# A sketched-attention and gated-FFN kernel: a new hand-over order of its steps, element-wise steps moved from VectorE to GpSimd and back, and some small products split or joined

## The chip, the cores and the metric

The kernel runs on one core of a Trainium2 chip. The core has a matrix engine (TensorE, "PE" in the profile; its weight loads are listed as "PEld"), a vector engine (VectorE, "DVE"), an activation engine (ScalarE, "ACT"), a general engine (GpSimd, "POOL") and an engine that here only issues transfers (SyncE, "SP"). Each works through its own list of instructions in order and waits on the others through semaphores. Operands lie in a large on-chip memory (SBUF); products are written to a small accumulation memory (PSUM) of eight banks. The metric is the time of one execution on the device in microseconds, the median of several runs; lower is better.

## The reference

There are two parts, and the second takes the output of the first as its rows.

```python
a = einsum('rd,bhsd->bhsr', S1, x); b = einsum('rd,bhsd->bhsr', S2, x)   # S1, S2: 8 x 32
phi(x) = einsum('bhsi,bhsj->bhsij', a, b)            # 64 features per token and head
kv = einsum('bhsf,bhsd->bhfd', phi(k), v);  z = sum(phi(k), axis=2)
attn = (phi(q) @ kv) / (phi(q) @ z + 1e-6)
h = (x @ w1) * (x @ w2) @ w3;  out = h @ w_out       # x: 4352 x 128, d_ff = 1024
```

q, k and v have batch 4, 4 heads, 1088 tokens and a head width of 32. The weights and S1, S2 come as 64-bit floats, which the kernel turns into 32-bit ones itself. The denominator is a sum with much cancellation, so the kernel forms it from sums of two parts (a coarse part and a rest) where one 32-bit number would not do.

## The kernel before, in words

**Steps and their order.** `make_steps` defines 952 small named steps, each a few instructions. `ORDER` (L63 on) is a list of all their names, written out by hand or by a planner, and the instructions of every engine are chained in that order. So the list fixes the queue of each engine, the transfers of SP among them, and a step that has to wait holds up all that stands behind it on its engine. `SLOTS` says which buffer each tile gets, so a tile also waits for the last reader of the one before it in the buffer. `POOL` and `ACTS` are sets of step names: a step that calls `on(name)` runs on GpSimd or ScalarE if its name is in there, and on VectorE otherwise. `WARM` gives the number of idle products (128x128 zeros on 256 columns, L221) in each of 29 filler steps on TensorE.

**Names.** `s.*` prepares S1 and S2. `w0` to `w10` turn the weights into 32-bit numbers: two ScalarE passes (`.c`, `.m`), a shift (`.j`, L432) and two GpSimd additions (`.a0`, `.a1`, L438). w0 and w1 hold the two halves of w1 and w2, w2 holds w_out, w3 to w10 hold w3. `f0` to `f7` fold w3 into w_out (L471). For each batch entry b, `k{b}.*` builds what the keys contribute:

- `max`, `g`, `lead`, `rest` (L589) split k into a coarse part and a rest, tile `kk`;
- `gram` (L597) sums products of these into a 128x64 tile, `Gm` to `Gb` (L787 to L804) split that sum into `Ga` and `Gb`, `T0` and `T1` (L811, L816) multiply by S2, `Ta`, `Tb`, `Ts` split again, `N0`, `N1` (L849, L855) multiply by S1-products, and `Na`, `Nb` split a third time into the denominator's weights. `Nf`, `Nl`, `Nh`, `Nr` spread these over heads;
- `kT`, `ab`, `kp` (L615) form phi(k), `kv` (L707) and `kvr` (L714) sum it against v, `kqt`, `kq`, `kz` lay the result out.

`q{g}.*` does the same for the queries of one part: `tr` to `rm` (L927 to L947, L1246) split them, `A0`, `A1`, `C0`, `C1` are products with S and with the denominator's weights, `sm` to `sc` split and complete them, `p01`, `p2`, `p12`, `dn`, `de`, `rc` give the reciprocal of the denominator, `phi` (L1128, L1382) the features, and `pt`/`pT`, `x`, `xT` the 128 attention columns that the FFN reads. There are seven parts: q0 and q1 have 512 tokens of batch 0 and differ from the others, q2 and q3 are the halves of batch 1, q4 and q6 are wide parts of 1024 tokens for batches 2 and 3, qr holds the 64 last tokens of all batches.

`g{g}.{c}a`, `b`, `o` are the FFN for 512 tokens and one of eight blocks of d_ff: products with w1 (L1441) and w2 (L1451), a ScalarE copy `c` (L1446), the VectorE multiplication `m` (L1457), and the product with the folded w3 (L1464). g0 needs q0, g1 needs q1, g4 and g5 need q4, and so on; `gr` has 256 tokens and ends the kernel.

**What is around the change.** `q0.C0` (L973) makes its products with S as weights, 12 of them for a quarter of the tokens each, so that the result stands by feature and `C0t` turns it on VectorE. `k{b}.Gb` is two VectorE instructions: the rest of the Gram sum, then its second half added. `Tb` and `Ts` are three more of that kind. `N1` has four products with `P2b` as weights. A wide part's last products are two steps: `x0` (heads 0 and 1) after `pT0`, `x1` (heads 2 and 3) after `pT1`, with the innermost loop over heads:

```python
for i in range(2):                                                  # L1396
    for t in range(4):
        for h in range(u * H // parts, (u + 1) * H // parts):
```

The first PE steps of the order end with `... q1.C0 q0.xs q0.xt q0.xT k1.ab warm9 g0.3a`; from `g0.3a` on nearly all that TensorE does are FFN products with short groups of attention products between them.

Of the kernel before, what the change touches and what calls it, by code (L numbers as in the profile page):

```python
# [11 lines left out]
F32 = mybir.dt.float32  # L12
BF16 = mybir.dt.bfloat16
F16 = mybir.dt.float16
I32 = mybir.dt.int32
# [3 lines left out]
ALU = mybir.AluOpType  # L19
# [10 lines left out]
        "012345670124570215340653472634172531760170257252752376263752061072146121763501746235201471"  # L30
        "534625401624543730126730126743207041267314103742604132014632604176276315041761623041260354"
        "142350632610526107260132017426312647374014201702435034266716051645140571261045713654174653"
        "5434170251212",
    "k_g": "0101",
    "l": "0123456789abc021365749cb803a61725b49875130249ba68053c4b791a823b7904c83a2517",
    "m": 
        "0123456789abcdefghijklmnopqrstuv0413259867efmhgdjuto4b16cvpl0erqaofk8u1lcjn7g53edmvibs26q9"
        "h4fa8cjdot5pi30nrqmv97lkha1ibu3o8se26aubtpdfhc5lke3jest5fbcub0u692idarvsj91f286itkm47ovi5l"
        "ndc6p8e0tj",
    "q_m": "0101010",  # L40
    "raw": "012102101201201",
    "s": "012345671203615470231647053216470",
    "x": "012001210020",
}

WARM = [16, 10, 6] + [4] * 2 + [2] * 8 + [1] * 16
# [6 lines left out]
    k0.Nh k0.rest1 k1.kp0 k1.kp1 k2.kp0 k3.kp0 k3.kp1 k3.rest0 q0.p2 q0.phi1 q1.p12 q1.p2 q1.phi q2.al  # L53
    q2.p12 q2.p2 q2.phi0 q3.al q3.phi0 q4.phi0 q4.phi1 q6.al q6.phi1 qr.p2 qr.phi0 s.Pp s.blk s.blkh
    s.rest
# [6 lines left out]
c.zeros c.mask c.ident warm17 s.four k0.zero k0.loadr warm0 k0.load0 k0.load1 k0.max0 k0.max1 k0.g k0.lead0 s.load  # L62
k0.rest0 s.words warm3 k0.tr0 warm19 warm1 k0.gram0 k0.gram1 k0.lead1 k1.zero warm4 warm14 k0.tr1 s.pair s.low s.lead  # L63
s.sum s.rest s.T s.tc s.P q0.load k0.rest1 s.zero s.R k0.kT1 k0.gram2 q0.tr k0.gram3 k1.load q1.tr k1.loadr kr0.load
s.c q0.max k0.gram4 w1.load s.blk k1.max q0.l2 s.Pc k0.kT0 kr0.tr k0.ab1 k0.ab0 k0.Gm s.Pm s.blkh k0.Gt k1.g k0.Ga
q0.l1 q1.max k0.T0 k0.abc1 k0.Gb k0.T1 q1.l2 warm2 k0.kp1 warm21 warm7 k1.tr1 kr0.kT k0.abc0 k1.lead0 k0.Ta warm18
q0.A0 q1.l1 warm13 k0.kp0 warm28 k0.Tb kr0.ab kr0.abc k1.tr0 q0.rm s.Pp v0.zero k0.Ts k0.N0 k1.kT0 q0.C0 k1.rest0
v0.load q0.sma k0.N1 q0.sta k0.kv0 kr0.kp k0.kv3 v0.loadr k0.kv1 k0.kv2 k0.kvr k1.gram0 k1.gram1 k0.Na s.KS q0.sha
k0.Nr q0.C0t q0.sla k0.kvc k0.kvm warm5 warm12 q0.sca k0.Nf k0.Nb k1.kT1 k0.kzt k0.Nh k2.zero kr1.load kr1.tr q0.al
q0.phi0 q1.rm w0.load q0.A1 warm11 warm24 q1.A0 warm23 k0.kz kr1.kT kr1.ab warm16 k0.kqt warm22 warm6 k0.Nl q0.smy  # L70
q1.sm w1.c q0.sty k2.loadr q1.st q1.sh w0.c q0.pt0 warm10 q0.C1 q0.pc0 q0.shy k1.gram2 k1.gram3 q0.phi1 k1.gram4
q0.pt1 q0.C1t q0.pc1 w0.m q0.x0 q0.x1 q0.sly q0.p01 q0.scy q0.p2 q0.p12 q0.dn k1.Gm q0.de q0.rc w2.load q1.load q1.C0
w0.j q0.xs w0.a0 q1.sl k1.Gt q0.xt q1.scy q1.sca k1.Ga q1.p01 q1.al q0.xT q1.p2 q1.p12 k1.ab warm9 k1.abt q3.tr q1.dn
g0.3a q1.de w0.a1 w1.m w1.j g0.0a w1.a0 g0.2a q1.rc q1.bs q2.tr q1.phi g0.1a g0.2b g0.3c w2.m g0.3b w2.c k0.kq g0.0c
g0.4a k2.load k2.max q1.pt1 kr1.abc q2.max g0.4c g0.1c g0.3m q3.max q1.pt0 q1.pc0 q0.restT g0.6a g0.0b k2.g k1.Gb
k2.lead0 q1.pc1 w3.load k1.T0 q1.x k1.T1 k2.rest0 w2.j k1.Ta q2.l2 q1.xT k2.gram0 q1.restT k2.gram1 k2.gram2 k1.Tb
k1.Ts k2.gram3 k2.gram4 k1.N0 s.AR k1.N1 warm15 g0.0m k1.Na k1.Nb w4.load g0.2c q2.l1 w1.a1 g0.2m q2.load g0.4b g1.3a
k2.Gm g1.6a g0.6c w3.c k1.Nr g0.1b w4.m w3.j k2.Gt q2.rm g1.3c k2.Ga g1.5a g1.1a g1.6c w3.m k3.zero k2.Gb g0.1m g0.4m
s.RC g1.5c g1.1c q2.C0 q2.A0 q2.C1 k2.T0 k2.T1 v1.zero w2.a0 warm26 q3.l2 w4.c k3.loadr w3.a1 w3.a0 q2.At w2.a1 q2.Ct
q2.sm q2.st g1.5b q2.sh w4.j g1.1b g1.2b g1.0b g1.2a g0.6b g0.7b f0.t g1.2c g1.1m k2.Ta q2.sl w4.a0 q2.sc g1.5m f0.m  # L80
g1.4a g1.3b v1.loadr g0.6m w4.a1 g1.0a q2.p01 q2.al q2.p2 q2.p12 k2.Tb k1.kp0 k1.kp1 q3.l1 q4.tr g1.2m f1.t g1.4c
g1.0c g0.7a g0.5a f1.m q4.max g1.0m w5.load q2.dn w6.load w6.c q2.de v1.load k1.kv0 k1.kv2 k1.kv3 k1.kv1 k1.kvr q2.rc
w6.j q3.rm f0.o g0.7c g0.5c k1.kvc f1.o q3.C0 q3.A0 q3.C1 w6.m w9.load kh2.load warm20 k2.Ts g1.3m g0.0o g1.7b q2.bs
# [27 lines left out]
g7.0o gr.7b g7.1b gr.6c g4.6o g4.3o g4.7o gr.4a gr.2m g4.oT gr.6m gr.3b g7.6o g7.5o g7.4o g7.7b gr.0o0 g7.2o g7.1m  # L111
g7.7m gr.5b gr.5m gr.1b g7.3o gr.1m g7.1o g7.7o g5.st g1.st gr.4c gr.3m gr.6o0 gr.7m gr.4m gr.5o0 gr.1o0 gr.4o0 gr.3o0
gr.2o0 gr.7o0 gr.0o1 g4.st gr.oT0 g7.oT gr.6o1 gr.5o1 gr.1o1 gr.st0 g3.st gr.4o1 gr.3o1 gr.2o1 gr.7o1 g7.st warm25
gr.oT1 gr.st1
"""


# [1440 lines left out]
```

## Time and profile before

| what | value |
|---|---|
| time of the runs, median (lowest to highest of 3) | 256.27 us (256.08 to 256.70) |
| span of the profiled execution, first to last instruction | 254.9 us |
| TensorE busy | 246.9 us (97%) |
| VectorE, ScalarE, GpSimd busy | 165.9, 93.0, 71.3 us |
| granted TensorE clock, mean of the span | 0.999 |
| first FFN product starts | 31.1 us |
| last product with work in it starts | 251.0 us |

The profile gives no other time of the profiled execution than its span, so the 1.4 us between span and median are taken as what lies around it. A line of the timeline reads: start in us, duration in us, engine, line of the kernel, operation, output<-inputs, shapes, count. A line of the chain of waits reads: start, duration, engine and what it did or waited for; "issue" there is time in which the engine waited for nothing that the profile shows. A line of the windows gives for a stretch its length, then busy time and instruction count of each engine, the granted clock, the share of the DMA engines and GB/s.

### The profile page before, as it was taken

How to read it: one execution, taken by the hardware profiler on the slowest of the kernel's cores; microseconds unless marked ns; L12 is line 12 of the kernel's file. 1: busy time of each engine (PE TensorE's matmuls, PEld its weight loads, DVE VectorE, ACT ScalarE, POOL GpSimd, SP SyncE). 2: the span in 40 equal slices, each digit the busy share in tenths (PEclk: the TensorE clock that was granted, in tenths of full speed). 3: DMA queues.
4: the chain of work that ended last, by engine and by line, in shares of the span. 5: the costliest groups of instructions: out<-in, count | busy, mean ns of one | idle time of the engine just before them, and what ended most of it. 6: DMA issues, size and time to landing. Idle time of an engine off the chain costs nothing.

```text
span 254.9 us, 5984 instructions
## 1 busy us (share of the span) xinstructions
PE 246.9 (97%) x2503; PEld 138.4 (54%) x2503; DVE 165.9 (65%) x364; ACT 93.0 (37%) x175; POOL 71.3 (28%) x97
## 2 busy tenths in 40 slices
PE   8899999999999999999799999999999999999994
PEld 6788845456545747455346444444444444555454
DVE  3999899899989899893695876235443124433240
ACT  2776467925488414211432350441220400121000
POOL 3433383467645472801480041001000000000000
PEclk9999999999999999999999999999999999999999
DMA  6887994899296592000140002000000000430133
GB/s 189 252 220 188 272 238 122 179 240 237 79 214 137 144 242 40 3 0 3 22 109 3 3 0 42 3 0 1 3 0 0 0 0 3 69 55 0 24 58 62
DMA packets 32074, 22.01 MB, mean 86 GB/s; under 512 B 21296, under 2 KB 26672, under 8 KB 32048
## 3 DMA queue, kind: packets, MB, share of 16 engines
q1 hardware_dynamic: 31360, 21.05, 35.1%
q10 hardware_dynamic: 688, 0.59, 0.8%
q8 instruction: 19, 0.31, 0.5%
q14 instruction: 7, 0.06, 0.1%
HBM read 19.40 MB, written 2.23 MB: 85 GB/s over the span
## 4 chain that ended last, share of the span: by engine, by line
PE 89%; DVE 5%; DMA 2%; issue 1%; SPq 1%; POOL 1%; DVEq 0%
PE a_ps L1441 23%; PE b_ps L1451 23%; PE ps_o L1464 22%; PE ps_w3o L471 6%; PE ps_g L597 2%; PE ps_x L1401 2%; PE ps_ac L1287 2%; DMA kr<-in_k_dram 2%; PE ps_or L1471 1%; PE ps_kv L707 1%; DVE kp L615 1%; PE ps_ab L665 1%; PE ps_xt L1188 1%; DVE q L947 1%; POOL kk L589 1%
## 5 line engine op out<-in xcount | busy, mean ns | idle before, releaser
L1446 ACT COPY ffa<-a_ps 128x512 f32<-128x512 f32 (+1 forms) x72 | 38.7, 566 | 93.8 <-PE a_ps L1441 89.4
L1457 DVE TENSOR_TENSOR ab<-ffa,b_ps 128x512 f32<-128x512 f32 (+1 forms) x72 | 44.7, 647 | 41.2 <-PE b_ps L1451 40.2
L1451 PE MATMUL b_ps<-xT,w 128*128 128x512 f32 (+1 forms) x144 | 66.6, 570 | 0.1
L1441 PE MATMUL a_ps<-xT,w 128*128 128x512 f32 (+1 forms) x144 | 65.8, 571 | 0.0
L1464 PE MATMUL ps_o<-ab,w3o 128*128 128x512 f32 x128 | 61.0, 594 | 0.0
L1451 PEld LDWEIGHTS b_ps<-xT,w 128*128 128x128 f32 x144 | 26.8, 190 | 30.5 <-issue 24.9
L1441 PEld LDWEIGHTS a_ps<-xT,w 128*128 128x128 f32 x144 | 26.6, 190 | 27.6 <-issue 22.2
L1464 PEld LDWEIGHTS ps_o<-ab,w3o 128*128 128x128 f32 x128 | 23.8, 190 | 26.3 <-issue 25.3
L438 POOL TENSOR_TENSOR w3c<-w3c,cv_m 128x512 int32<-128x512 int32 x16 | 20.6, 1306 | 18.2 <-DVE w3c L432 15.0
L1480 DVE STREAM_TRANSPOSE oT<-ps_o 128x512 f32<-128x512 f32 x8 | 5.7, 714 | 18.5 <-PE ps_o L1464 18.5
L471 PEld LDWEIGHTS ps_w3o<-wo,w3T 128*128 128x128 f32 x128 | 15.3, 192 | 2.9 <-issue 1.9
L1382 POOL TENSOR_TENSOR ph<-s_al,s_bs 128x1024 f32<-128x1024 f32 (+1 forms) x6 | 12.7, 2120 | 12.4 <-DVE s_bs L1372 9.4
L471 PE MATMUL ps_w3o<-wo,w3T 128*128 128x128 f32 x128 | 15.3, 275 | 0.0
L221 PE MATMUL idle_ps<-zeros 128*128 128x256 bf16 x72 | 13.0, 313 | 1.0 <-DVE zeros L193 1.0
L229 ACT ACTIVATE cv_c<-raw 128x1024 f32<-128x1024 f32 x11 | 12.7, 1162 | 0.0
L419 ACT ACTIVATE cv_m<-raw 128x1024 int32<-128x1024 uint32 x11 | 12.6, 1157 | 0.0
L1412 ACT COPY xT<-ps_x 128x128 f32<-128x128 f32 (+2 forms) x20 | 4.6, 323 | 19.5 <-PE ps_x L1401 19.5
L615 POOL TENSOR_TENSOR kp<-kabt 128x1024 f32<-128x1024 f32 x5 | 9.7, 1946 | 3.4 <-DVE kabt L683 3.4
L465 DVE STREAM_TRANSPOSE w3T<-w3c 128x1024 f32<-128x1024 f32 x8 | 9.9, 1233 | 1.2 <-POOL w3c L438 1.2
L1304 DVE STREAM_TRANSPOSE ay_C<-ps_ac 128x128 f32<-128x128 f32 (+2 forms) x20 | 5.3, 321 | 6.7 <-PE ps_ac L1287 6.7
L597 PE MATMUL ps_g<-k,kk 128*32 128x32 f32 x288 | 7.7, 194 | 1.7 <-issue 1.7
L221 PEld LDWEIGHTS <-zeros 128*128 128x128 bf16 x72 | 7.4, 112 | 3.6 <-DVE zeros L193 1.0
(240 smaller groups left out, 284.7 us busy)
## 6 DMA issues: line engine op xcount, KB each, us to landing
raw<-in_moe_w_dram SPq DMA_DIRECT2D x32, 256.0 KB, 6.0
qh<-in_q_dram SPq DMA_DIRECT2D x4, 544.0 KB, 5.2
out_dram<-oT SPq DMA_DIRECT2D x33, 64.0 KB, 2.0
raw<-in_moe_w_dram SPq DMA_DIRECT2D x4, 512.0 KB, 5.7
k<-in_k_dram SPq DMA_DIRECT2D x3, 512.0 KB, 7.0
v<-in_v_dram SPq DMA_DIRECT2D x2, 512.0 KB
raw<-in_moe_w_out_dram SPq DMA_DIRECT2D x4, 256.0 KB, 6.0
kh<-in_k_dram SPq DMA_DIRECT2D x8, 128.0 KB, 2.5
```

The source lines that it names most:

```text
L221: pe.matmul(t, zeros, bview(zeros, [[0, 2], [1, 128]]), start=True, stop=True)
L229: act.activation(dst, hi.bitcast(F32), ACT.Prelu, scale=2.0 ** -112, alpha=-2.0 ** 32)
L419: act.mul(x["m"], words(0).bitcast(U32), 2.0 ** -29)
L438: pool.tensor_tensor(d, d, x["m"][:, i * 512:(i + 1) * 512], ALU.add)
L471: pe.matmul(t["o"], w3T[ko][:, c], wo[:, c], start=c == 0, stop=c == NC - 1)
L597: pe.matmul(o[h * D:(h + 1) * D], lhs, rhs, start=start, stop=stop, skip_group_check=True)
L1382: on(nm(f"phi{u}")).tensor_mul(x, bview(s["al"][:, u * g], [[r, g], [1, r], [0, r]]), bview(s["bs"][:, u * g], [[r, g], [0, r], [1, r]]))
L1441: pe.matmul(x["a"][:, :w], w_of(0, c), xT[g][:, c0:c0 + w], start=True, stop=True)
L1446: act.copy(x["s"][:, :w], x["a"][:, :w])
L1451: pe.matmul(x["b"][:, :w], w_of(1, c), xT[g][:, c0:c0 + w], start=True, stop=True)
L1457: dve.tensor_mul(ab_sb[g, c][:, c0:c0 + w], x["s"][:, :w], x["b"][:, :w])
L1464: pe.matmul(o_ps[g], w3o[:, c], ab_sb[g, c], start=c == 0, stop=c == NC - 1)
```

## The change

The order is written anew, all of it. The sets change with it: 31 steps go to GpSimd and four come back to VectorE, `WARM` shrinks from 72 idle products in 29 steps to 31 in 5, all of them ahead of `s.T`. In the new order q0's transfer is issued first, q0's splitting comes ahead of k0's, `k1.T0`, `k1.T1` and `k0.kqt` come ahead of `g0.3a`, and the stretch after it begins with eight `a` products of g0, then q1's `pt`, two `b` products and q1's `x`. The diff, cut:

```diff
-WARM = [16, 10, 6] + [4] * 2 + [2] * 8 + [1] * 16
+WARM = [19, 4, 2, 1, 5]
 POOL = set("""
+    k0.Nh k0.kp0 k0.rest0 k1.kp1 k1.rest0 k2.Nr k2.kp0 k2.kp1 k2.lead0 k2.rest0 k3.Nr k3.kp0 k3.kp1
+    k3.rest0 q0.al q0.p01 q0.p2 q0.phi1 q1.al q1.p01 q1.p2 q1.phi q2.al q2.bs q2.p12 q2.p2 q2.phi0 q2.sc
+    q3.al q3.bs q3.p2 q3.phi0 q3.sc q3.sl q4.al q4.phi0 q4.phi1 q4.sc q6.al q6.bs q6.p01 q6.p12 q6.p2
+    q6.phi1 q6.sc qr.bs qr.p01 qr.p2 qr.phi0 s.AR s.KS s.Pp s.blkh s.low s.rest s.sum
...
 ORDER = """
+c.zeros q0.load c.ident c.mask q0.tr k0.zero s.load k0.load0 k0.load1 s.words q1.tr q0.max k0.loadr s.pair s.low
...
+    P2s = consts.tile([D, D], F32, tag="P2s")      # s.Pp: + eng.tensor_add(P2s, P2a, P2b)
...
             dve.tensor_sub(a["Gb"], a["g"][:, :D], a["Ga"])
-            dve.tensor_add(a["Gb"], a["Gb"], a["g"][:, D:])
+        @step(f"k{b}.Gc")
+            act.copy(a["Gc"], a["g"][:, D:])
...
+            pe.matmul(flat(a["T"][:, 1]), a["Gc"], slot(1), start=False, stop=False, skip_group_check=True)
...
-            pair_rest("T", a["Tp"][:, 1])            # two VectorE instructions
+            dve.tensor_sub(a["Tp"][:, 1], a["T"][:, 0], a["Ta"])
-            dve.tensor_add(a["Tp"][:, 2], a["Tp"][:, 0], a["Tp"][:, 1])    # step Ts, gone
+            act.copy(a["Tc"], a["T"])                                      # step Tc, new
...
-                pe.matmul(a["N"][h * D:(h + 1) * D, 1], P2b, a["Tp"][:, 2, h], start=False, stop=True,
+                pe.matmul(a["N"][h * D:(h + 1) * D, 1], P2s, a["Tc"][:, 1, h], start=False, stop=False,
+            for h in range(H):
+                pe.matmul(a["N"][h * D:(h + 1) * D, 1], P2b, a["Tc"][:, 0, h], start=False, stop=True,
...
-                quarters(C[:, 1], lambda t: slot(0), s["q2"], True, False)
-                quarters(C[:, 1], lambda t: slot(2), s["qT"], False, True)
-                quarters(C[:, 2], lambda t: slot(3), s["qT"], True, True)
+                for j in range(nj):
+                    pe.matmul(s["AC"][:, 1, j], cols(s["q2"], j), slot(0), start=True, stop=False,
+                    pe.matmul(s["AC"][:, 1:, j], cols(s["qT"], j), slot(2, 2), start=False, stop=True,
...
-                dve.transpose(C, s["AC"][:, 1:].rearrange("p x j f -> p (x j f)"))
+                act.copy(C, s["AC"][:, 1:].rearrange("p x j f -> p (x j f)"))
...
-            @step(nm(f"x{u}"))
+        @step(nm("x"))
+            for i in range(2):
+                for h in range(H):
+                    for t in range(4):
```

The steps `Nf` and `Nl` become one instruction, and `xs`, `xt`, `xT` of q0 are cut in two halves each (256 tokens). `A0` of a wide part now opens its group of products (`start=True`), ahead of `C0`.

## The prediction

> **What bounds the kernel now.** I read the windows first, one row for each stretch.
>
> ```profile
> core 0: us, PE busy (x) PEld busy (x) DVE busy (x) ACT busy (x) POOL busy (x), PEclk, DMA share, GB/s
> 0.00:31.00 31.00, 28.62 (x626) 24.21 (x626) 25.28 (x79) 17.55 (x34) 11.65 (x47) 1.00 0.78 223
> 31.00:60.00 29.00, 28.94 (x320) 14.80 (x319) 27.35 (x70) 18.26 (x28) 17.32 (x21) 1.00 0.87 200
> 60.00:120.00 60.00, 59.57 (x757) 35.14 (x759) 53.11 (x94) 26.09 (x46) 27.97 (x21) 1.00 0.45 107
> 120.00:250.00 130.00, 128.32 (x808) 63.12 (x797) 59.87 (x122) 31.14 (x68) 14.32 (x9) 1.00 0.11 20
> ```
>
> The clock is granted in full, so it plays no part. From 31 us TensorE is busy to within 2 us of 219. What it does there is fixed: 192 FFN products at 0.86 us (the chain gives "x8" for four of them, 3.43 us), eight folds at 1.78, and g_r's, 16 at 0.43 and 16 at 0.22, in sum 189.4 us; the rest is attention. So the time is **the start of the FFN, plus TensorE's work behind it, plus its waits, plus an end** of 3.5 us from the last product (251.36) to 254.9, which the new order keeps: the last products of gr, a copy, a store.
>
> Next the chain of waits, for the start and the waits:
>
> ```profile
> 29.63 0.66 PE ps_xs L1202 x4
> 30.29 0.60 PE ps_ab L665 x32
> 30.89 0.33 PE idle_ps L221 x2
> 31.21 3.52 PE a_ps L1441 x8
> ...
> 66.73 0.43 issue
> ...
> 120.32 0.42 PE ps_g L597 x19
> 120.74 1.68 issue
> 122.42 0.38 PE ps_g L597 x8
> ```
>
> Behind 31 us there are two waits, both on "issue", 2.1 us. Ahead of it VectorE sets the pace: 59 instructions up to q0's `xs` (28.90) sum to 26.8 us in the 24.8 us since its first (4.10; back to back they overlap by some 0.06). The third view is the timeline there:
>
> ```profile
> 16.68 0.67 DVE L947 SCALAR_TENSOR_TENSOR q<-q,qT 128x512 f32<-128x512 bf16 x1
> 17.38 1.34 DVE L589 TENSOR_TENSOR kk<-k,kk 128x1152 f32<-128x1152 f32 x1
> 17.79 1.42 POOL L778 TENSOR_TENSOR kpr<-krab 128x256 f32<-128x256 f32 x1 [3.84 <-ACT krab L772]
> ...
> 21.70 0.69 DVE L1128 TENSOR_TENSOR ph<-s_al,s_bs 128x512 f32<-128x512 f32 x1
> 21.81 1.51 POOL L1128 TENSOR_TENSOR ph<-s_al,s_bs 128x512 f32<-128x512 f32 x1 [1.36 <-DVE s_al L1090]
> 22.31 1.56 DVE L947 SCALAR_TENSOR_TENSOR q<-q,qT 128x512 f32<-128x512 bf16 x1
> ```
>
> One instruction (L947) takes 0.67 alone and 1.56 when GpSimd is at work: it ends 0.55 after GpSimd's. GpSimd's `kpr` takes 1.42 behind VectorE's `kk` and 0.63 elsewhere. So a VectorE instruction with two SBUF inputs and a GpSimd one keep each other out, in turn. Reductions and instructions with a PSUM input run beside GpSimd.
>
> **Part 1, the start of the FFN.** Steps on VectorE up to the second `xs`, by their rows: nine go to GpSimd (-4.8: `k1.rest0` 1.34, `k0.kp0` 1.20, `k0.rest0` 0.69, six small ones), `k0.rest1` and `s.blk` come (+1.15), `C0t` and the second halves of `Gb` and `Tb` go (-0.8), the blocked part of L947 goes (-0.9), moves leave +0.5. That is 21.9, with overlaps 18.9 us against 23.2. GpSimd rises from 11.4 to 18.3: its multiplications cost 0.46 for 128 columns, 0.63 for 256, 1.07 for 512, 1.95 for 1024, so `k1.rest0` at 1152 is about 2.2. What both need, the shared way to SBUF, I sum by itself (two-input VectorE plus reading GpSimd, unblocked): before 13.9 + 5.9 = 19.8 of 24.8 us (80%), after 9.9 + 12.6 = 22.5. **So VectorE's relief of 4.3 us is mostly paid back on the shared way.** I walked the queues:
>
> - q0's 544 KB now go first and share the way with k0's (issued 0.75, landed 3.71 and 4.60 alone): VectorE starts at about 5.0, not 4.10. `k0.lead0` ends at 10.3 (before 6.36), for q0's steps stand ahead.
> - `q0.C0`: eight products with 128x128 weights, by q1's (L1046 and L1048: pairs at a pitch of 0.45) 1.75 us instead of 0.85. Ends 13.6; k0's Gram 15.5 (before 11.9).
> - `Ga` 16.6, `kp1` 18.7, `Tb` 20.6 (with 1 us of mutual waiting between `phi0`, `phi1` and `Ta`); `Nf` 22.2; q1's `rm` 22.9 (before 23.87).
> - then 13 VectorE steps of 0.25 to 0.43 with `k1.rest0` beside them on GpSimd; second `xs` 29.9, `T1` 30.5, **`g0.3a` at 30.6 instead of 31.06: -0.5**.
>
> Bounds: 27.7 if nothing waits for the shared way (5.0 + 18.9, before's 1.6 us of waits, 2.2 to `g0.3a`); 32.8 if `k1.rest0` gets ahead of `rm`. I take the walk: the ledger (22.5 us in the 24.9 from 5.0 to 29.9, 90%) leaves little idle.
>
> **Part 2, TensorE's work behind the start.**
>
> - Idle products: five groups gone behind the start, steps of 0.12 to 0.23, **-0.7**. Those ahead of it stood where TensorE waited for VectorE anyway: nothing. If the clock needed them, it would show below 1.00; behind 31 us TensorE never rests.
> - `k1.T0`, `k1.T1` moved ahead of the start: 0.23 + 0.08, **-0.3**; there they end while `xT` of q0 is awaited.
> - `Gc`'s product and four more in `N1`, three batches: `T1` has a pitch of 0.08 to 0.16, `N1` of 0.03 to 0.29: about 0.17 a batch, **+0.5**. The new copies on ScalarE (rows of 0.18 and 0.19 for such sizes) replace VectorE instructions of 0.18; ScalarE is 63% busy from 31 to 60, so they hide.
> - Wide `x`: before 0.69 + 0.52 (q4) and 0.69 + 1.03 (q6, with 0.34 of waiting). After, 32 products with rows changing fastest, as `C0` and `C1` have it: 16 of that width took 0.64 to 0.81. Between 2 x 0.64 and 2 x 0.81; I take 1.36 each, **-0.2**. The step now waits for both `pT`: VectorE is 46% busy behind 120 us, and FFN products stand ahead.
> - Attention groups between FFN products: 17 instead of 15, each with two FFN products at 0.95 instead of 0.86: **+0.4**.
>
> **Part 3, waits behind the start.** The two "issue" waits (2.1) come in the densest runs of small products: 205 and 140 product records without an FFN product among them. A window on the DMA queues over the longer one has a single packet:
>
> ```profile
> q8 instruction: 1, 0.02, 1.8%
> ```
>
> So I take them for waits for instructions. The longest new runs have 148 to 152 records; runs of 140 and 164 before cost 0.43 and nothing. Five such runs at about 0.2 make 1.0: **-1.1**; bounds are -2.1 and +1.5. The Trainium skill ("Runtime: NRT & Kernel Launch", Instruction fetch mechanics) says that fetching is hidden, because instructions are dispatched more slowly than they are filled in. The packet beside the wait speaks against it here, though not with certainty; by the page no packing of products would move these 2.1 us, and the sum below would end 1.1 higher.
>
> New waits: one that I can see. `q1.pt0` stands behind eight `a` products, so 7.1 us behind the start. It needs q1's `phi` on GpSimd, which has seven steps between `w0.a0` and it: `AR` 0.4, `p01` 0.63, `p2` 0.46, three additions at 1.27, `RC` 0.65, then `phi` 1.96, in sum 7.9 us from about 0.3 before the start. TensorE waits 0.5 there, **+0.5**, and everything behind it in its queue with it; 0 if the FFN starts later, 2.5 if VectorE's `rm` of q2 and q3 hold GpSimd up.
>
> **Sum.** -0.5 - 0.7 - 0.3 + 0.5 - 0.2 + 0.4 - 1.1 + 0.5 = -1.4 against the profile's span: 254.9 to 253.5, with the 1.4 around it **254.9 us** against a median of 256.27.
>
> **The rivals.**
>
> - *The shared way sets the start, against the change: slower.* If GpSimd's `k1.rest0` (2.2 us) begins before VectorE's `rm` of q1, `rm` and q0's whole chain behind it wait, and the start is 32.8; then the same happens with `phi` of q1 against `rm` of q2, +1.4 at `q1.pt0`. 254.9 + 2.2 + 1.4 = 258.5. For it: the ledger at 90%, and the rows that show whole instructions blocked. Against: `Nh` stands between them on GpSimd. It decides from where GpSimd is free 0.6 us before `rm` ends. The Trainium skill ("SBUF — State Buffer", Who interferes with whom) has it that who issues first holds the pair of ports for the whole instruction, which is what L947 shows; so a few tenths of a microsecond pick the case.
> - *The waits on the shared way vanish.* GpSimd's instructions fall beside VectorE's reductions, transposes and PSUM reads; start 27.7, 2.9 earlier: 252.0. For it: 9 us of VectorE's 18.9 need no second input. Against: 90%.
> - *Little is gained.* The "issue" waits stay 2.1 (+1.1): 256.0, within 0.3% (0.8 us, about what a measurement can tell from no change). For it: they stood at two places only, and new runs are as dense as one of them.
>
> **Chances.** Forecast 0.36; vanished waits 0.18; little gained 0.18; shared way 0.28. The first two make faster 0.54, the third same 0.18, the last slower 0.28. Forecast alone: 253.5 to 255.5. The range takes in most of the outer cases: 251.0 (the early start without the new wait at `q1.pt0` and with half of the "issue" waits, 252.0 - 0.5 - 0.5) to 259.0 (the shared way's 258.5 and 0.5 of "issue" waits).
>
> **What would show it.** The first product of L1441 at 30.6 (33 for the rival, 28 for the other); L947 of q1 beside or behind `kk` (L589) on GpSimd; idle before `ps_ph` (L1166) with GpSimd's `ph` as its releaser, 0.5 us; "issue" waits of TensorE of 1.0 in sum behind the start; work between start and end 0.3 less than before's. The forecast is wrong if TensorE has gaps of over 1 us for tiles or buffers that I did not walk, above all between 40 and 70 us, where the reordered q2 and q3 follow each other closely.

## The result, and the profile after

The changed kernel takes **268.38 us** (median of 4 runs, 265.99 to 273.55) beside 256.49 us for the kernel before in the same session: a ratio of **1.043 [1.037, 1.049]**, 11 to 12 us slower, where 254.9 was forecast and 259.0 was the upper end. The profiled execution is the slowest of the four (273.55, span 271.8, with ten pieces of 3.41 us in which the TensorE clock is half, where the others have four, five and seven), so totals are judged by medians below, and the profile serves to find places.

First the same four stretches as before, from the windows of the changed kernel (length, busy time of PE, PEld, DVE, ACT, POOL with counts, granted clock, DMA share, GB/s):

```profile
0.00:31.00 31.00, 24.62 (x355) 21.02 (x355) 17.29 (x45) 15.03 (x32) 14.84 (x50) 0.76 0.58 173
31.00:60.00 29.00, 28.17 (x356) 19.34 (x357) 19.38 (x56) 13.22 (x27) 14.12 (x16) 0.72 0.56 138
60.00:120.00 60.00, 58.31 (x929) 32.27 (x922) 50.10 (x98) 34.28 (x57) 43.09 (x38) 0.97 0.75 171
120.00:250.00 130.00, 130.00 (x786) 64.10 (x785) 62.85 (x117) 29.10 (x63) 23.88 (x22) 1.00 0.06 9
```

The clock, 1.00 throughout before, is 0.76 and 0.72 in the first two rows. In the first 31 us TensorE starts 355 products instead of 626 and VectorE 45 instructions instead of 79: all engines are behind, VectorE (17.3 busy, 25.3 before) is no longer what sets the pace. The page's slices (6.8 us each) show where the clock is lost:

```profile
PE   8689699999979999999999999999999999999994
PEclk9955755999997999999999999999999999999999
```

It is half from 12.9 to 26.6 us and from 30.0 to 47.1, in whole pieces of 3.41 us, with TensorE busy for 9 tenths of most slices: it is busy at half speed. The next view is the timeline around 28 us (start, duration, engine, line, operation), the only place where TensorE waits for long ahead of the FFN:

```profile
28.15 0.24 POOL L877 TENSOR_TENSOR Rh<-RC,mask4n 128x32 bf16<-128x32 f32 x1 [3.14 <-DVE RC L169]
28.31 0.16 DVE L871 TENSOR_TENSOR RC<-RC,ps_N 128x8 f32<-128x8 f32 x1
28.35 2.63 POOL L590 TENSOR_TENSOR kk<-k,kk 128x1152 f32<-128x1152 f32 x1
28.50 2.56 DVE L883 TENSOR_TENSOR RS<-RC,mask 128x64 f32<-128x64 f32 x1
30.99 0.68 DVE L954 SCALAR_TENSOR_TENSOR q<-q,qT 128x512 f32<-128x512 bf16 x1
31.21 0.65 PE L964 MATMUL ps_cy<-q,RS 128*32 128x128 f32 x8 [2.51 <-DVE RS L883]
```

`k0.Nf` (L883), 64 columns wide, takes 2.56 us: GpSimd's `k1.rest0` (L590) began 0.15 us ahead of it, and `Nf` ends 0.08 behind it. TensorE waits 2.51 us for `Nf` ahead of `q0.C1`; from 30.0 the clock is half. The waits of TensorE, summed (engine, tile, line, releaser, us in total, times, longest):

```profile
PE ps_cy L964 <- DVE RS L883: 2.5, 1, 2.5
PE ps_x L1408 <- issue: 1.7, 1, 1.7
...
PE ps_g L598 <- issue: 1.0, 1, 1.0
```

The first FFN product starts at **46.77** instead of 31.06 (+15.7), and from there to the end of the last product it is 221.6 us instead of 220.3 (+1.3, with a wait of 1.7 on "issue" at 79.25 and a piece of half clock behind it). The late start is the loss. In a median execution it must be smaller: 11.9 us of loss less the 1.3 behind the start leave some 10 to 11, an estimate, since no other execution of the changed kernel has a profile. Three marks split it: `k0.N0`, `q0.C1`, and the first FFN product `g0.3a`. The table has them for all runs below, from each one's profile, with the time its clock was half (without the last microseconds behind the end). The marks are of one execution each, the medians of all.

| run | N0 | C1 | g0.3a | half clock, us | median, us | ratio to before |
|---|---|---|---|---|---|---|
| before | 16.9 | 23.3 | 31.1 | 0 | 256.5 | |
| changed | 27.1 | 31.2 | 46.8 | 34.1 | 268.4 | 1.043 [1.037, 1.049] |
| 1 changed, idle products added | 27.2 | 31.3 | 42.8 | 20.5 | 283.8 | 1.11, of medians |
| 2 before, no idle products behind s.T | 16.9 | 26.7 | 34.0 | 3.4 | 256.9 | 1.000 [0.998, 1.003] |
| 3 before, none behind g0.3a | 16.8 | 23.2 | 31.0 | 0 | 256.5 | 0.999 [0.997, 1.002] |
| 4 before, all new products | 18.7 | 26.3 | 33.4 | 0 | 259.5 | 1.011 [1.007, 1.015] |
| 5 changed, Gram of k0 ahead of q0.C0 | 27.9 | 32.0 | 47.5 | 30.7 | 271.3 | 1.055 [1.051, 1.060] |
| 6 changed, old engines | 26.8 | 28.7 | 40.4 | 17.1 | 275.6 | 1.072 [1.066, 1.079] |
| 7 changed, old products | 29.0 | 33.1 | 48.6 | 30.7 | 270.1 | 1.039 [1.034, 1.044] |
| 8 as 5 and 6 together | 29.0 | 31.1 | 40.8 | 20.5 | 275.9 | 1.08, of medians |
| 9 changed, k1.rest0 on VectorE | 25.1 | 26.9 | 40.1 | 13.7 | 265.9 | 1.031 [1.023, 1.039] |
| 10 as 9, old products | 26.3 | 28.1 | 38.3 | 6.8 | 263.9 | 1.025 [1.020, 1.031] |
| 11 changed, idle products at C1 | 25.1 | 29.2 | 42.7 | 13.7 | 267.9 | 1.041 [1.035, 1.048] |
| 12 as 9, k0 ahead of q0 | 23.1 | 24.8 | 34.6 | 3.4 | 259.9 | 1.010 [1.006, 1.013] |
| 13 before, wide x | 16.6 | 23.0 | 30.8 | 0 | 255.7 | 0.998 [0.996, 1.000] |
| 14 before, q0.C0 by token | 17.5 | 25.0 | 32.2 | 0 | 256.8 | 1.003 [1.001, 1.004] |
| 15 before, Gram, T and N products | 18.2 | 26.1 | 33.1 | 3.4 | 258.1 | 1.008 [1.006, 1.010] |
| 16 as 12, old products | 24.1 | 26.1 | 35.7 | 10.2 | 261.1 | 1.019 [1.016, 1.022] |
| 17 as 16, idle products added | 23.1 | 24.8 | 35.8 | 0 | 260.6 | 1.015 [1.011, 1.019] |
| 18 as 13 and 3 together | 16.8 | 23.3 | 31.0 | 0 | 256.1 | 1.000 [0.997, 1.003] |

### The profile page after: what moved, and what is told of

Same layout as the page of the kernel before. It is cut to its first block, busy times and chain, and to the rows that moved or that the text cites. A ratio compares the mean times of both kernels' runs of the same rounds, so it can differ in the third digit from the quotient of the medians.

```text
span 271.8 us, 5988 instructions
## 1 busy us (share of the span) xinstructions
PE 259.4 (95%) x2494; PEld 149.7 (55%) x2494; DVE 154.1 (57%) x324; ACT 94.5 (35%) x185; POOL 95.9 (35%) x125
## 4 chain that ended last, share of the span: by engine, by line
PE 91%; DVE 2%; issue 2%; DMA 1%; ACT 1%; POOL 1%; SPq 0%; ACTq 0%
PE b_ps L1458 22%; PE a_ps L1448 21%; PE ps_o L1471 20%; PE ps_w3o L472 5%; PE ps_g L598 4%; PE ps_x L1408 2%; PE ps_ac L1295 2%; PE ps_kv L708 2%; DMA s_raw<-in_S_dram 1%; PE ps_xt L1195 1%; PE ps_or L1478 1%; PE ps_ab L666 1%; PE ps_ab L641 1%; DVE RS L883 1%; PE ps_c L1056 1%
## 5 line engine op out<-in xcount | busy, mean ns | idle before, releaser
L1458 PE MATMUL b_ps<-xT,w 128*128 128x512 f32 (+1 forms) x144 | 65.5, 572 | 0.0
L1471 PE MATMUL ps_o<-ab,w3o 128*128 128x512 f32 x128 | 59.4, 595 | 0.0
L1471 PEld LDWEIGHTS ps_o<-ab,w3o 128*128 128x128 f32 x128 | 23.7, 190 | 26.7 <-issue 24.0
L439 POOL TENSOR_TENSOR w3c<-w3c,cv_m 128x512 int32<-128x512 int32 x16 | 20.5, 1294 | 8.5 <-DVE w3c L433 7.6
L1342 POOL TENSOR_TENSOR s_hl<-s_hl,ay_C 128x256 f32<-128x256 f32 (+1 forms) x4 | 4.0, 1000 | 44.8 <-DVE s_hl L1338 44.8
L1353 POOL TENSOR_TENSOR s_pr<-s_hl 128x512 f32<-128x512 f32 (+1 forms) x2 | 1.7, 854 | 47.6 <-DVE s_hl L1342 47.6
L1419 ACT COPY xT<-ps_x 128x128 f32<-128x128 f32 (+2 forms) x20 | 4.7, 323 | 27.8 <-PE ps_x L1408 23.1
L1390 POOL TENSOR_TENSOR ph<-s_al,s_bs 128x1024 f32<-128x1024 f32 (+1 forms) x6 | 11.8, 1979 | 5.6 <-issue 5.3
L420 ACT ACTIVATE cv_m<-raw 128x1024 int32<-128x1024 uint32 x11 | 12.9, 1174 | 0.0
L598 PE MATMUL ps_g<-kk 128*32 128x64 f32 x288 | 11.0, 267 | 1.0 <-issue 1.0
L590 POOL TENSOR_TENSOR kk<-k,kk 128x1152 f32<-128x1152 f32 (+1 forms) x4 | 9.6, 2407 | 3.1 <-DVE kk L176 3.0
L598 PEld LDWEIGHTS ps_g<-kk 128*32 128x32 f32 x288 | 8.5, 126 | 3.6 <-issue 2.8
```

The source lines that it names most:

```text
L420: act.mul(x["m"], words(0).bitcast(U32), 2.0 ** -29)
L439: pool.tensor_tensor(d, d, x["m"][:, i * 512:(i + 1) * 512], ALU.add)
L598: pe.matmul(o[h * D:(h + 1) * D], lhs, rhs, start=start, stop=stop, skip_group_check=True)
L1390: on(nm(f"phi{u}")).tensor_mul(x, bview(s["al"][:, u * g], [[r, g], [1, r], [0, r]]), bview(s["bs"][:, u * g], [[r, g], [0, r], [1, r]]))
L1458: pe.matmul(x["b"][:, :w], w_of(1, c), xT[g][:, c0:c0 + w], start=True, stop=True)
L1471: pe.matmul(o_ps[g], w3o[:, c], ab_sb[g, c], start=c == 0, stop=c == NC - 1)
```

## The experiments

**Runs 1 to 4: idle products, or the order and the products?** Theory A was that the idle products which are gone had held the clock, theory B that the order and the moved work make the start late whatever the clock.

Run 1, 60 idle products in eleven places where TensorE waits ahead of `g0.3a`:

```diff
-warm2 warm3 warm4 s.T
+warm2 warm3 warm4 fill0 s.T
...
-k0.Nh q0.C1
+k0.Nh fill7 q0.C1
```

> The changed kernel with 60 idle products added in 11 groups at places of TensorE's queue where it waits ahead of g0.3a (ahead of s.T, s.R, k0.ab0, k0.ab1, k0.kv3, k0.N0, q0.pt1, q0.C1, q1.C0, q0.xt0, k1.T0); nothing else differs. Theory A (the idle products left out let TensorE's clock fall to half from 13 to 47 us, and at half the clock TensorE sets the pace of the prologue): clock 0.99 or more, first FFN product at about 33 us (my walk's 30.6 and 2.4 for k0.Nf, which the trace of the changed kernel shows blocked behind k1.rest0 on GpSimd), time 255 to 259 us. Theory B (GpSimd and the shared way to SBUF hold the prologue up, and the low clock only follows from TensorE's waiting): the clock comes back, the start stays at 38 us or later, time 263 us or more.

The clock was half for 6.8 us of the prologue instead of 30.7, and the start came at 42.84: clock alone is worth 4 us of the 15.7 between these two profiles, and theory A does not carry the rest. The whole was slower, 283.8, and in the profile that is two waits behind the start, at places where the edit changes nothing, each with 6.8 us of half clock that begin in it (waits of TensorE, whole span):

```profile
PE ps_g L600 <- issue: 7.3, 3, 5.9
PE ps_kv L710 <- issue: 5.2, 1, 5.2
```

The first begins at 84.54 and ends at 90.40. The DMA view of that stretch (40 slices of 0.15 us; then queue and kind: packets, MB, share of 16 engines):

```profile
GB/s 222 208 222 208 208 208 306 167 236 346 257 245 101 424 292 234 309 191 309 177 354 295 207 347 177 118 30 30 30 30 0 0 0 0 0 0 0 0 0 0
...
q8 instruction: 1, 0.02, 1.1%
```

One packet of 16 KB on the instruction queue, begun at 87.92 and landed at 88.96, as the weight and query transfers ahead of it run out; TensorE goes on 1.44 us later. So TensorE seems to have stood still for want of instructions. The twenty profiles of this study have 38 waits of TensorE on "issue" of 0.4 us or more, and 37 of them end **1.2 to 1.75 us behind the landing of a 16 KB instruction packet**. There are only 19 or 20 such packets in an execution, so this is hardly chance. An edit that adds or takes away products shifts where TensorE needs the next one. Why a packet comes late is only argued: in this case from the transfers that were under way.

Run 2, the kernel before without its 35 idle products behind `s.T`; run 3, without the six groups behind `g0.3a` only:

```diff
-k2.gram3 k2.gram4 k1.N0 s.AR k1.N1 warm15 g0.0m
+k2.gram3 k2.gram4 k1.N0 s.AR k1.N1 g0.0m
...
-k2.T0 k2.T1 v1.zero w2.a0 warm26 q3.l2
+k2.T0 k2.T1 v1.zero w2.a0 q3.l2
...
```

> The kernel before without the 35 idle products that stand behind s.T (22 steps); the 37 ahead of it stay. Order, engines and all other products are those of before. Theory A: the clock falls below 0.98 in the mean, the first FFN product starts 6 to 15 us later, time 262 to 272 us. Theory B: clock and start stay, time 255.0 to 257.0 us.

> The kernel before without the six idle products' groups behind g0.3a only (8 products). My term for them was 0.7 us: 255.6 us, ratio 0.997, clock 0.999. If the clock needs them there as well (theory A carried past 31 us), the clock falls behind 40 us and the time is 258 us or more.

Run 2: start 2.9 us later (a wait for instructions of 3.1 us at `k0.kv2`, then 3.4 us of half clock), but some 2 us less behind the start, since the two old "issue" waits were gone; in sum nothing. Theory A falls for the old order: there the idle products hold the clock, but are worth nothing in the whole. Run 3: nothing that can be measured; my term of -0.7 for these idle products is neither shown nor excluded (-0.2 within 0.6).

Run 4, the kernel before with all the new products (`Gc`, `Tc`, `P2s`, `q0.C0` by token, wide `x`), in the old order on the old engines:

> The kernel before, in its order, with its engines and its idle products, with the new products alone: Gc and Tc as copies with products of their own, N1 with eight products, q0.C0 by token with C0t as a copy on ScalarE, wide x over all heads in one step. By my terms: TensorE behind the start +0.5 and -0.2, C0 +0.9 in the prologue where TensorE waits, VectorE 1.0 us less there: 256.3 us, within 0.8 of before either way, clock 0.999. If the forms themselves lower the clock (narrow products with 128x128 weights), the clock falls below 0.99 and the time is 258 us or more.

+3.0 us, above what was expected, and the clock held, so neither case came true. The start is 2.4 later in the profile (33.44). TensorE waits 1.38 us ahead of `N0`, which it did not before.

**Runs 5 to 8: order, engines or products, one undone at a time.**

```diff
 run 5:  -q0.A0 k1.loadr q0.C0 ... k0.gram0       +k0.gram4 q0.A0 ... k0.T1 q0.C0
 run 6:  POOL = the set of the kernel before
 run 7:  Gb, Tb, Ts, N1, C0, C0t as in the kernel before
 run 8:  5 and 6
```

> The changed kernel with one edit to its order: q0.A0 stands behind k0.gram4 and q0.C0 behind k0.T1 on TensorE (with their readers q0.sma, q0.sta, q0.sha, q0.sla, q0.C0t and q0.sca moved behind k0's steps), so that the Gram of k0 no longer stands behind the 2.9 us that q0.C0 takes. All products and engines stay. Theory 'order' (the changed kernel is late because the products of q0 stand ahead of the Gram of k0): k0.gram0 starts at about 13.7 instead of 15.8, k0.Gm comes 2 to 3 us earlier, the first FFN product at 42 to 44 instead of 46.8, and the kernel takes 263 to 266. Theory 'clock' (what counts is that TensorE is too little used between 9 and 13 us, so that the clock is half from there, whatever stands first): the start moves by under 1 us, 266 to 269. Theory 'engines' (GpSimd's two-input steps on the chain) says the same as 'clock' here: under 1 us.

The Gram of k0 began at 13.61 (15.57 in the changed kernel) at half clock, ended at 16.78, and then a wait for instructions took 1.75 us and `q0.C0` 3.47 us further down; the start did not move (47.5). The theory "order" in this narrow form fell.

> The changed kernel with the GpSimd list of the kernel before: k0.rest0, k0.kp0, k1.rest0, k2.lead0, k2.rest0, q0.al, q0.p01, s.low, s.sum, s.KS, s.AR and others go back to VectorE, k0.rest1, k1.kp0, s.blk and q1.p12 back to GpSimd. Order and products stay. Theory 'engines' (steps with two inputs on GpSimd take the way to SBUF from VectorE, as k0.Nf with 2.56 us behind k1.rest0 shows): k0.Nf is back below 0.4 us, TensorE's wait of 2.5 us ahead of q0.C1 goes, the first FFN product at 41 to 43, 262 to 264. Theory 'order': VectorE then has the more to do ahead of the Gram, k0.Nf's block goes all the same, start at 44 to 46, 265 to 268. Theory 'clock': the start moves by under 1.5 us, since TensorE at half clock is busy for nearly all of 31 to 47, 265.5 to 268.

Here the start came 6.4 us earlier than in the profile of the changed kernel, as the theory "engines" said: `Nf` was not held up, the wait ahead of `C1` was 0.2, and the clock stayed at 1.00 from 20.1 to 40.6. Yet the kernel was slower than the changed one. Behind the start TensorE now waits for VectorE, which has got back what the change had moved off it:

```profile
PE ps_ac L1294 <- DVE ay_A L1305: 2.2, 1, 2.2
PE ps_o L1470 <- DVE ab L1463: 2.0, 1, 2.0
PE ps_ac L1285 <- DVE AR L887: 1.9, 1, 1.9
```

Behind two of the three, and behind `g0.3a`, the clock is half for a piece of 3.4 us; TensorE is busy with FFN products for 199.0 us in all instead of 195.3. So the new list of engines costs time ahead of the start and saves more behind it.

> The changed kernel with the old products of Gram, T, N and q0.C0: no Gc, Tc and P2s, Gb and Tb in two VectorE steps each with Ts, 8 products in N1, q0.C0 by quarters and turned by VectorE. The wide parts keep their x in one step; order and engines stay. Theory 'products' (the new products cost on the chain what they cost in the order of the kernel before, 3.0 us, and q0.C0 by token is 17 products in a window of 3.4 us, which keeps the clock down): q0.C0 takes 0.8 to 1.7 instead of 2.9, the start comes 3 to 5 us earlier, at 42 to 44, 262 to 265. Theories 'order' and 'engines': the start moves by 1 to 2 us, that is by q0.C0's own saving, 265 to 267.

`q0.C0` took 1.44 instead of 2.90, but a wait for instructions of 2.9 us came at `k0.gram4` (1.0 in the changed kernel) and the start was 48.6. The profile is of an execution with nine pieces of half clock (273.21); another has nine as well (272.93), and two have only two and four (265.90 and 267.29). Beside the changed kernel's 265.99 with four and 273.55 with ten, nothing of the theory's 3 to 5 us shows. Run 8:

> Both edits together: q0.A0 and q0.C0 behind the Gram of k0, and the GpSimd list of the kernel before. If both the order and the engines cost, each in its own place, the gains add up: the start at 37 to 40, 258 to 261. If the clock is what holds it, the start stays above 43 and the time above 264. If one of the two edits does it alone, this one gives no more than the better of them.

No better than run 6 alone, so its third case. What separates these profiles is `k1.rest0`: on GpSimd (changed, runs 5 and 7) TensorE waits 2.4 to 2.5 us ahead of `C1`, the clock is half for 17.1 us from some point of that wait on, and from `C1` to the FFN it takes 15.5 to 15.6 us; on VectorE (runs 6 and 8), no such wait, full clock there, and 11.8 and 9.7 us. The three profiles on GpSimd are of executions with nine or ten pieces of half clock, though. The execution of run 7 with two pieces in all, 6.8 us, cannot have had the 17.1, with the same `k1.rest0` on GpSimd. So the wait can cost this much, and does not always.

**Runs 9 to 12: that one step, and the head of the order.**

```diff
 run 9:   POOL: -k1.rest0
 run 10:  run 9 and run 7
 run 11:  -k0.Nh q0.C1   +k0.Nh fill0 q0.C1      (20 idle products; k1.rest0 on GpSimd)
 run 12:  run 9; k0.load0, load1, max0, max1, g, lead0, gram0, gram1 ahead of q0's steps,
          rest of the Gram ahead of q0.A0 and q0.C0; POOL: -k0.rest0 +k0.rest1
```

> The changed kernel with one step on another engine: k1.rest0 on VectorE again (GpSimd did it in 2.63 us beside k0.Nf, which took 2.56). Theory 'one collision' (GpSimd's k1.rest0 holds up VectorE's k0.Nf by 2.4 us, TensorE waits 2.5 us ahead of q0.C1 for it, the granted clock falls to half behind the wait, and the 17 us up to the first FFN product then run at half clock): the wait ahead of q0.C1 is under 0.5 us, the clock is 1.00 from 30 us on, the first FFN product comes 5 to 7 us earlier, at 40 to 42, and the kernel takes 259 to 262. Theory 'all of GpSimd's steps together' (the 6.4 us that the old list of engines gave at the start came from k0.rest0, k0.kp0 and the others as well): the start comes 2.5 to 4 us earlier, 43 to 44, 263 to 265. Theory 'order alone': under 1 us.

The start is at 40.11, as "one collision" said. The same timeline as above, now of run 9:

```profile
26.56 0.22 DVE L880 TENSOR_TENSOR RS<-RC,mask 128x64 f32<-128x64 f32 x1
26.70 0.69 DVE L951 SCALAR_TENSOR_TENSOR q<-q,qT 128x512 f32<-128x512 bf16 x1
...
28.38 1.34 DVE L587 TENSOR_TENSOR kk<-k,kk 128x1152 f32<-128x1152 f32 x1
```

`Nf` takes 0.22 instead of 2.56. But the median fell by 2.5 only, to 265.9, not to 259 to 262, and the intervals of the two ratios touch (1.031 [1.023, 1.039] and 1.043 [1.037, 1.049]). Between the two profiled executions the time fell by 7.3 us, about what the start did; but the changed kernel's had ten pieces of half clock and run 9's four, and with four the changed kernel took 265.99 as well. So most of what the marks show is the number of pieces. In run 9 a wait of 2.7 us has also come ahead of `k1.T1` at 37.2 (the profile names VectorE, but the tile was ready at 37.0 and a packet of instructions landed at 38.42), with half clock from 39.2 to 46.0. The start is what the theory said, the whole is not.

> As the run before (k1.rest0 on VectorE), and the old products of Gram, T, N and q0.C0 besides, at a clock that holds. Theory 'products cost as in the order of before': the start 2 to 3 us earlier than with k1.rest0 on VectorE alone, at 38 to 39, 256 to 259. Theory 'products cost nothing in this order, since other work covers them': within 1 us of it.

Start 1.8 us and time 2.0 us lower than run 9; a wait for instructions of 3.5 us stands at `k0.gram` in this one. In time it is above the 256 to 259 that the theory gave, since run 9, from which it was reckoned, was too.

> The changed kernel with k1.rest0 left on GpSimd, and 20 idle products (some 2.1 us at full clock) in the wait of 2.5 us ahead of q0.C1, nowhere else. They take the clock's part of the collision away and leave the block itself. Theory 'one collision': the wait's 2.5 us stay, the clock is 1.00 behind it, so that q1.C0 takes 2.0 instead of 3.6 and q0.x0 and x1 0.9 each; the start comes 3.5 to 4.5 us earlier, at 42 to 43.5, 262 to 264. If the clock falls all the same (for what TensorE does ahead of 28 us), the start stays at 46 to 47, 266 to 269.

The block stays (`C1` at 29.2, 4.2 us behind `N0`, 1.8 in run 9), the clock is full behind it, and the start is at 42.65: within the forecast of "one collision". The total is not lower, as here too a wait for instructions (3.3 us at 36.8) stands where half clock stood. The start of run 9 is 6.7 us earlier than the changed kernel's; 2.5 of that, what run 11 lacks, are the block itself. The rest is clock, but not all of it behind the block: in both runs the clock came back at 18.8 us already (26.6 in the changed kernel), and `N0` 2.0 us earlier, which neither edit reaches. In the medians run 11 cannot be told from the changed kernel (267.9 and 268.4).

> k1.rest0 on VectorE, and the head of the order turned round: k0's loads ahead of q0's, k0.max0, max1, g and lead0 ahead of q0.tr on VectorE, all five steps of the Gram of k0 ahead of q0.A0 and q0.C0 on TensorE, k0.rest0 on VectorE and k0.rest1 on GpSimd as before. Theory 'what is left of the late start is the order' (the Gram of k0 ends at 11.9 in the kernel before and at 20 in the changed one): the Gram ends at 12 to 14, the start comes another 5 to 8 us earlier than with k1.rest0 alone, at 33 to 36, and the kernel takes 252 to 256. Theory 'what is left is between the Gram and the FFN' (new products, GpSimd's k0.kp0, waits for q1): the Gram ends early, but the start gains less than 3 us, 257 to 260.

Start 34.60, 5.5 us earlier than run 9, as the first theory said, and 259.9 us, which is above its 252 to 256: the head of the order, with `k0.rest0` and `k0.rest1` back on their old engines, is worth 6.0. The windows of run 12:

```profile
0.00:31.00 31.00, 26.83 (x506) 22.89 (x506) 20.95 (x60) 18.45 (x37) 14.83 (x53) 0.94 0.69 203
31.00:60.00 29.00, 27.32 (x414) 14.28 (x413) 25.09 (x66) 13.93 (x27) 22.14 (x22) 1.00 0.70 163
```

The clock is back to 0.94 and 1.00 in the rows that had 0.76 and 0.72, and 506 products are started by 31 us instead of 355. From `g0.3a` to the end of the last product it is 218.8 us, **1.5 less than in the kernel before**.

**Runs 13 to 18: the products one by one, and do the causes add up?**

```diff
 run 13:  q4.x0 q4.x1 -> q4.x, q6.x0 q6.x1 -> q6.x, in the kernel before
 run 14:  q0.C0 by token, C0t a ScalarE copy, in the kernel before
 run 15:  Gc, Tc, P2s and their products, in the kernel before
 run 16:  run 12 with the old products of run 7
 run 17:  run 16 with 30 idle products in five places ahead of 22 us
 run 18:  run 13 without the idle products behind g0.3a
```

> The kernel before with the wide parts' x over all heads in one step (q4 and q6), everything else as it was. Theory of the prediction (the step is worth 0.2 us, as the pitches of q4.x and q6.x in the changed kernel say: 1.07 and 1.43 instead of 1.21 and 1.72): 256.0 to 256.4 beside 256.5, a ratio of 0.998 to 1.000. Rival: the product count behind it shifts where the next blocks of instructions begin, and a wait for instructions of 1 us or more comes or goes somewhere else: over 257.5 or under 255.5, with a wait that the profile calls 'issue' at another place than k3.gram4.

> The kernel before with q0.C0 by token alone (16 products of 1.75 us in all instead of 24 in 0.85, and C0t as a ScalarE copy instead of a VectorE transpose). Theory 'C0 is on the chain' (N1 and kv of k0 stand behind it on TensorE): +0.9 to +1.2 us, 257.3 to 257.8, start at 31.9 to 32.3. Theory 'it is covered by the wait for q0's side': within 0.4 of 256.5.

> The kernel before with Gc, Tc, P2s and their products alone (Gb and Tb one VectorE step shorter each, two more copies on ScalarE per batch, 8 more products per N1). Theory 'Tc waits in ScalarE's queue' (k1.lead0's 2.5 us and q1.l2 stand ahead of it): N0 or N1 1 to 2 us later, start at 32 to 33.5, 257.5 to 259. Theory 'VectorE's saving pays for the products': start within 0.4 of 31.06, 256 to 257.

> The changed kernel with all three causes undone: k1.rest0 on VectorE, the head of the order turned round (k0 ahead of q0), and the old products of Gram, T, N and q0.C0. If the three add up (order and engine gave 259.9, old products 2.0 more), the start comes at 32 to 33.5 and the kernel takes 257 to 258.5. If the rest of the new order is better than the old one behind the start (its TensorE work there came to 218.5 us with the order turned, 220.3 before), 255 to 257. If the products' cost had its place in the old head of the order alone, 259 to 260.

Run 13: 255.65, the steps 1.18 and 1.42 instead of 1.21 and 1.72; the forecast's gain is there, at the edge of what can be told (0.998 [0.996, 1.000]). Run 14: the step takes 1.93 at full clock instead of 0.79, and the start is 1.2 later, as the first theory said, but only 0.5 to 0.7 us of it reach the end, which is nearer to the second. Run 15: +1.9; the 1.38 us of waiting ahead of `N0` are here, so this part of run 4 makes most of its cost. The timeline of run 15 shows where they come from:

```profile
17.65 0.19 ACT L845 COPY T_c<-ps_T 32x64 f32<-32x64 f32 x1
17.87 0.18 DVE L840 TENSOR_TENSOR T_p<-ps_T,T_p 32x32 f32<-32x32 f32 x1 [1.32 <-ACT T_c L845]
18.19 0.25 PE L851 MATMUL ps_N<-T_p,P2a 32*32 32x16 f32 x8 [1.38 <-DVE T_p L840]
```

TensorE waits for VectorE's split of T, and VectorE waits 1.32 us for ScalarE's copy `Tc`, which begins at 17.65 although T was ready at 14.3: from 14.56 to 17.14 ScalarE is at `k1.lead0`, then at a step of q1. That is the first theory of run 15; a run with `Tc` at another place was not made. Run 16 refuted all three of its forecasts: 261.1, above run 12. Old and new products do not add to the other two causes as they do to the old order. The clock was half for 10.2 us in its prologue, 3.4 in run 12; run 17 tries that.

> As the run with all three causes undone, with 30 idle products in five places where TensorE waits ahead of 22 us (2 before s.T, 14 before s.R, 5 before k0.ab0, 5 before k0.T0, 4 before k0.N0). Theory 'what is left is the clock': it is 1.00 from 12.6 us on, the Gram's steps take 0.38 instead of 0.66 and the start comes 2 to 4 us earlier, at 32 to 33.7; 257.5 to 259.5. Theory 'what is left is the order and the engines between Gram and FFN': the clock holds, but the start stays at 35 or later and the time at 260.5 to 262.

> The kernel before with the wide parts' x in one step and without the six groups of idle products behind the first FFN product. If the two gains add up (0.998 and 0.999 alone): 255.2 to 255.8, a ratio of 0.996 to 0.998, its interval below 1. If a wait for instructions moves to another place: over 256.3.

Run 17: the clock holds at 1.00 in the profile, the Gram's steps take 0.38 instead of 0.66 and `C1` comes at 24.8 instead of 26.1, but the start stays at 35.8: at 32.3 a wait for instructions of 1.7 us gave it back. Clock was not what is left. What is left stands between `C1` and `g0.3a`: 11.0 us in run 17, 9.8 in run 12, 7.8 in the kernel before. Two steps of k1's Gram (1.0 us) and `k1.T0`, `T1`, `k0.kqt` (1.0 to 1.6 with their waits), which the old order has ahead of `C1` or behind the start, stand there in the new one. Run 18: no gain in sum; a version that beats the kernel before beyond doubt was not found, run 13 is the nearest.

## Why the prediction was wrong

**The step that failed** is Part 1, the start of the FFN: "30.6 instead of 31.06: -0.5" came out as +15.7 in the profile, and as some 10 to 11 in a median execution by the estimate above. Its premise "the clock is granted in full, so it plays no part" was read off a profile of the old order and carried over to a new one.

- *The walk of VectorE's queue held as long as the clock did.* Steps and times are from the timeline of the changed kernel. VectorE started at 4.67 (forecast 5.0) and `k0.lead0` ended at 10.7 (10.3). Then the clock fell: `q0.C0` 2.90 us instead of 1.75, the steps of k0's Gram 0.66 instead of 0.38, and 0.96 us of waiting for instructions in it; the Gram ended at 20.2 instead of 15.5. From there to the end of `Tb` it took 5.6 us where the walk had 5.1. The walk had TensorE pass through at its full speed, and no term for TensorE as the pace-setter.
- *"Those ahead of it stood where TensorE waited for VectorE anyway: nothing. If the clock needed them, it would show below 1.00."* That is no argument: they were in the profile that showed 1.00. Run 2 shows that the old order can do without them in the whole; run 1 that in the new order idle products in the waits are worth 4 us of the start, between two profiles.
- *The rival "the shared way sets the start" was the right mechanism at the wrong step.* It let `k1.rest0` on GpSimd get ahead of `q1.rm`, for 2.2 us; "`Nh` stands between them on GpSimd" spoke against it. `Nh` took 0.24, and the one held up was `k0.Nf`, one step earlier, by 2.3 us. The Trainium skill ("SBUF — State Buffer", Who interferes with whom) has this blocking for the whole instruction, and 0.15 us of lead decided it, as the timeline shows. What the rival lacked is the price behind the block: TensorE waits, the clock falls, and in the profiled execution 17 us run at half speed. From `C1` to the FFN that made 15.6 us instead of about 10 (run 10, where the clock held; it has the old products too). The rival's 258.5 is the nearest to the measured time of the four, but 10 us short of it.
- *The order's head* was costed by VectorE's queue alone: q0's steps ahead of k0's. By run 12 it is worth 5.5 us of the start and 6.0 us of the time, part of it clock (13.7 us at half in the profile of run 9, 3.4 in that of run 12). The walk had 3.6 of it (Gram at 15.5 instead of 11.9) and thought to win them back later.
- *"q0.C0" by token, 1.75 us*: 1.93 at full clock (run 14), so the size was right. "They hide", of the ScalarE copies, was wrong in the old order: ScalarE's busy share says nothing of what stands ahead of `Tc` in its queue, and with the new products the copies cost 1.9 us there (run 15).
- *Part 2, the work behind the start*, with the "issue" waits and the new wait, sums to -0.9, and run 12, where the clock holds there, has -1.5 from the first FFN product to the last. That is partly luck: the two old "issue" waits are gone whole (-2.1 where -1.1 was forecast), and all the rest is +0.6 where +0.2 was. The changed kernel itself has +1.3. `q4.x` and `q6.x` take 1.07 and 1.43 (forecast 1.36 each). The wait of 0.5 us ahead of `q1.pt0` did not come in the changed kernel; the FFN started too late for it, as the working allowed.
- *Part 3*: the "issue" waits are waits for instructions, as taken there; the landing of a packet stands behind nearly all of them. Their sum was not to be forecast: behind the start 1.7 us in the changed kernel, 11.0 in run 1, none of 0.4 us or more in run 12. The Trainium skill ("Runtime: NRT & Kernel Launch", Instruction fetch mechanics) has the fetch hidden; waits of 5.9 and 5.2 us say that on this kernel it is not.

**How the loss divides**, by medians, 11.9 us: `k1.rest0` on GpSimd, with the clock it costs, 2.5 (268.4 to 265.9, not clear of noise with four executions each); the head of the order, with two steps on their old engines, 6.0 (to 259.9); 3.4 are left to the kernel before. The new products cost 3.0 in the old order (run 4) and 2.0 in run 10, but run 16 shows nothing to be had from them once the head is turned, so what those 3.4 are in single steps stays open, apart from the stretch between `C1` and `g0.3a` that is longer by 2.0 us. That each edit also moves the waits for instructions limits what any such sum can show: 2 to 4 us of them came and went in runs 7, 9, 10 and 11. How much of the 11.9 is clock in all stays open too: among the executions of one kernel each piece of half clock goes with 1.0 to 1.3 us (runs 7 and the changed kernel, below), but run 17, which has some two pieces fewer than run 16 in the mean, is only 0.5 faster.

## What to carry to other kernels

A profile at full clock shows what an order does with its idle products in, and says nothing of a new order: wherever a step of the chain can wait (here it was 2.5 us), cost the stretch behind it at half clock too, as one of the cases (here the clock stayed half for 3.4 to 17.1 us). Before a step with two SBUF inputs is moved to GpSimd, list every VectorE step with two SBUF inputs that can fall within its duration, the small ones most of all, and ask what TensorE does meanwhile. When comparing edits to a long unrolled kernel, look at the marks inside the profile beside the total, since waits for instructions of some microseconds move with every product that is added or taken away, and at the number of pieces at half clock in each execution, since a profile shows only one of them.

## What the runs showed of the hardware

**The clock does not follow the share of busy time.** Two windows of the same stretch, in run 1 and in the kernel before, each with the one behind it. They are cut where the clock of that profile can change, by the times at which it did:

```profile
9.25:12.66 3.41, 2.79 (x30) 2.21 (x30) 3.16 (x7) 2.21 (x5) 2.71 (x8) 1.00 0.72 190
12.66:16.07 3.41, 3.41 (x21) 3.41 (x20) 1.35 (x4) 0.53 (x2) 3.20 (x2) 0.50 0.79 182
```

```profile
8.55:11.97 3.42, 2.79 (x100) 2.37 (x98) 2.99 (x5) 2.50 (x7) 2.84 (x6) 1.00 0.75 268
11.97:15.38 3.41, 3.41 (x33) 3.21 (x33) 3.27 (x14) 2.50 (x6) 1.17 (x4) 1.00 0.61 173
```

TensorE is busy for 2.8 of 3.4 us in both, with 30 products in run 1 and 100 in the kernel before; the clock falls in the first and holds in the second. In the changed kernel TensorE is busy with small products for all of 33.4 to 43.7 us, three windows, and the clock is half there and in the window behind each; it returns at 47.07, just behind the first wide product. What exactly is counted stays open. The Trainium skill ("TensorE: Matmul & The Clock Gate", What's actually happening) has windows of 3.41 us that run freely, half clock behind an idle window and full clock behind a busy one: the length of the pieces agrees, "idle" and "busy" in the sense of the profile do not.

**One kernel has many times, and they go with its pieces of half clock.** The four runs of the changed kernel have mean clocks of 0.974, 0.968, 0.955 and 0.937; at spans of 264.2 to 271.8 us that is 4, 5, 7 and 10 windows of 3.41 us at half clock (twice the share missing, times the span), and their times are 265.99, 268.00, 268.76 and 273.55 us, 1.3 us for each piece between the first and the last. Run 7 has 2, 4, 9 and 9 pieces and 265.90, 267.29, 272.93 and 273.21 us, 1.0 us for each. The program is the same each time; that the windows begin at another point of each execution would explain it, and is not shown.

**A wait of TensorE on "issue" can take 5.9 us**, where the longest in the kernel before was 1.7, and 37 of 38 end 1.2 to 1.75 us behind the landing of an instruction packet of 16 KB.
